# Results of the first four blocks copied out of PSUM by ScalarE, one block's taps back on VectorE, and the first loads in one ring

## The chip, the cores and the metric

The kernel runs on one core of one Trainium2 chip. The metric is the device time of one execution in microseconds (us); the kernel before has a median of 696.08 us in 5 runs (695.95 to 696.86). [...] Transfers issued by SP and ACT go through hardware queues, those issued by POOL through one software queue, called the ring here; all run on the core's 16 DMA engines.

## The reference

A light convolution along the sequence, then a two-layer network with exact GELU. Cut to what matters:

```
x: 8 x 4096 x 192;  weight: 8 heads x 7;  w_in: 192 x 2048;  w_out: 2048 x 192
w   = softmax(weight, over the 7 taps)
y[b, s, c] = sum over k of w[head(c), k] * x[b, s - 6 + k, c]     (zero before s = 0)
h   = y @ w_in                       (32768 tokens)
out = (0.5 * h * (1 + erf(h / sqrt 2))) @ w_out
```

## The kernel before

**Tiling.** The 32768 tokens are two halves of 16384, worked on side by side: the partitions 0 to 63 hold channels of the first half, 64 to 127 those of the second, and the 192 channels are three parts p of 64. Each half is cut into 34 blocks (`WS`): blocks 0 to 3 have 256 tokens of each half, blocks 4 to 33 have 512. Blocks are counted from 0 in this text. Matmuls come in pairs, one on each half of the rows of the array.

**A block's way.** (1) Four transfers (L182) bring x into `xin`, three buffers in turn. (2) VectorE transposes it into `xT`, three instructions (L390), and GpSimd copies the 6 tokens of overlap, the halo (L270, L281, L287). (3) The 7 taps: in most blocks VectorE takes them, 3 multiplications (L413) and 18 multiply-adds (L420), each over one p, the last three writing the bf16 tile `xc`. In the blocks listed in `PC` (0, 1 and 3) TensorE takes them instead, with diagonal matrices `dg`: `xT` is cast to bf16 (L502 on ScalarE for block 0, L365 on VectorE for blocks 1 and 3), 14 matmuls for each p (`pconv`, L564) add the taps in PSUM, and `xc` is copied from there (L510 on ScalarE for block 0, `conv_out`, L373, on VectorE for 1 and 3). (4) `mm1` (L602) multiplies `xc` by W_in into one of two PSUM tiles `hp`, one slice at a time: 8 slices in a block of 256, 16 in one of 512. (5) ScalarE applies GELU to each slice (L531) and writes `gT`. Slice u may enter its `hp` only after the GELU of slice u-2. (6) `mm2` (L636) multiplies `gT` by W_out into one of two PSUM tiles `ob`; a block is a row of units of two matmuls, 32 units to a group of 128 tokens per half: 64 units in a block of 256 tokens, 128 in one of 512. (7) `evac` (L429) on VectorE copies a finished group from `ob` to `osb`, 128x384 in f32, and SP stores it (L196).

**Order of the work.** It is written out by hand for each engine, and each engine works strictly in that order. TensorE goes through the slices of block n and, behind each slice, through some units of block n-1; the list `share` says how many for blocks 1 and 2, and elsewhere they are spread evenly. `behind` sets the `pconv` of block 1 behind slices 2, 4 and 6 of block 0, and that of block 3 behind slices 1, 2 and 3 of block 2. VectorE goes through 24 operations of each block (3 transposes, 21 taps); the list `side` puts other work in front of operation o of block b, written (b, o): the `conv_out` of block 1 at (2, 1), (2, 4) and (2, 8); transposes, casts and `conv_out` of block 3 in block 4; and each `evac`, for example that of block 0's first group at (2, 20). An `evac` waits for its group's last matmul, and what stands behind it on VectorE waits with it.

**The first loads.** SP loads half of block 0's x, ACT the other half; SP then waits for the first piece of W_in, loads half of block 1's x, waits for W_out, and loads blocks 3, 4 and so on. POOL's ring carries, in order: W_in's first quarter of a half (`win_in`, L236), then after an `affine_select` its second, the other half of block 1's x, then after the halo of block 0 the last piece of W_in, block 2's x, and W_out (L296). Each W_in piece fills one half of the partitions for its columns; `dup` (L350) on VectorE copies it to the other half. VectorE has `dup(0)`, `dup(1)`, the transposes and casts of block 1, then `dup(2)`, which slice 4 of block 0 needs.

The functions that the change touches, and what calls them:

## Time and profile before

| | |
|---|---|
| median of 5 runs | 696.08 us (695.95 to 696.86) |
| the profiled execution: its time | 696.08 us |
| its span in the profile | 694.2 us |
| TensorE clock granted | 1.00 |
| TensorE busy / ScalarE / VectorE | 685.6 / 528.3 / 552.7 us |
| HBM read / written | 52.92 / 25.17 MB |

The profile is of one execution. The span runs from its first to its last instruction; the execution's time holds 1.88 us more. A line such as "L531 ACT" is source line 531 on ScalarE; a row of the timeline gives start, length, engine, line, operation and count, and in brackets the idle time before it with what ended it. "x12" of L602 in a block of 256 tokens is one slice, "x6" in one of 512. The span of a group of matmuls there holds a tail that the next group overlaps; the chain of waits counts each stretch of time once, so lengths of TensorE's work are taken from the chain.

### The profile page before, as it was taken

How to read it: one execution, taken by the hardware profiler on the slowest of the kernel's cores; microseconds unless marked ns; L12 is line 12 of the kernel's file. 1: busy time of each engine (PE TensorE's matmuls, PEld its weight loads, DVE VectorE, ACT ScalarE, POOL GpSimd, SP SyncE). 2: the span in 40 equal slices, each digit the busy share in tenths (PEclk: the TensorE clock that was granted, in tenths of full speed). 3: DMA queues.
4: the chain of work that ended last, by engine and by line, in shares of the span. 5: the costliest groups of instructions: out<-in, count | busy, mean ns of one | idle time of the engine just before them, and what ended most of it. 6: DMA issues, size and time to landing. Idle time of an engine off the chain costs nothing.

```text
span 694.2 us, 25348 instructions
## 1 busy us (share of the span) xinstructions
PE 685.6 (99%) x11598; PEld 503.6 (73%) x11598; DVE 552.7 (80%) x915; ACT 528.3 (76%) x524; POOL 43.2 (6%) x93
## 2 busy tenths in 40 slices
PE   8899999999999999999999999999999999999997
PEld 4787677777777777777777777777777777777777
DVE  6898977789777889778898777898877898777811
ACT  6669877777777777777777777777777777777771
POOL 6100000000000000000000000000000000000000
PEclk9999999999999999999999999999999999999999
DMA  9858443445543355543355543355533455521013
GB/s 198 175 138 201 107 117 80 95 123 137 137 107 91 89 128 138 137 104 86 91 133 137 138 101 84 92 137 137 136 96 86 96 138 137 135 49 33 17 47 94
DMA packets 23082, 78.15 MB, mean 113 GB/s; under 512 B 6976, under 2 KB 11200, under 8 KB 19136
## 3 DMA queue, kind: packets, MB, share of 16 engines
q1 hardware_dynamic: 18640, 73.03, 44.0%
q0 software_dynamic: 3600, 2.73, 2.4%
q8 instruction: 91, 1.49, 0.9%
q10 hardware_dynamic: 736, 0.78, 0.4%
q14 instruction: 15, 0.12, 0.1%
HBM read 52.92 MB, written 25.17 MB: 112 GB/s over the span
## 4 chain that ended last, share of the span: by engine, by line
PE 96%; DMA 2%; DVE 1%; POOL 1%; ACT 0%; issue 0%
PE ob L636 49%; PE hp L602 47%; DMA xin<-in_x_dram 2%; PE ob L564 0%; ACT gT L531 0%; DVE xT L390 0%; POOL xin L182 0%; DVE acc L413 0%; POOL xTb L281 0%; POOL win L236 0%; ACT L488 0%; DVE acc L420 0%; DVE xc L373 0%; DVE osb L429 0%
## 5 line engine op out<-in xcount | busy, mean ns | idle before, releaser
L531 ACT ACTIVATE gT<-hp 128x1024 bf16<-128x1024 f32 x512 | 522.7, 1023 | 147.5 <-PE hp L602 147.3
L636 PEld LDWEIGHTS ob<-wout,gT 64*128 64x128 bf16 x8192 | 352.4, 94 | 115.7 <-PE ob L636 0.9
L636 PE MATMUL ob<-wout,gT 64*128 64x192 bf16 x8192 | 420.4, 243 | 0.2
L602 PE MATMUL hp<-xc,win 64*128 64x512 bf16 (+1 forms) x3264 | 415.1, 363 | 3.3 <-DVE xc L373 1.3
L420 DVE SCALAR_TENSOR_TENSOR acc<-xT,wcol,acc 128x512 f32<-128x512 f32 (+1 forms) x465 | 311.3, 732 | 0.0
L602 PEld LDWEIGHTS hp<-xc,win 64*128 64x128 bf16 x3264 | 150.1, 94 | 64.3 <-ACT gT L531 3.4
L429 DVE COPY osb<-ob 128x384 f32<-128x384 f32 x128 | 70.4, 550 | 130.9 <-PE ob L636 130.9
L390 DVE STREAM_TRANSPOSE xT<-xin 128x512 f32<-128x512 f32 (+1 forms) x102 | 61.2, 650 | 3.2 <-DMA xin<-in_x_dram 3.1
L420 DVE SCALAR_TENSOR_TENSOR xc<-xT,wcol,acc 128x512 bf16<-128x512 f32 (+1 forms) x93 | 63.4, 734 | 0.0
L287 POOL COPY xT<-xT 128x558 f32<-128x558 f32 x31 | 20.2, 652 | 578.5 <-DVE xT L390 578.5
L413 DVE TENSOR_SCALAR acc<-xT,wcol 128x512 f32<-128x512 f32 (+1 forms) x93 | 54.2, 633 | 1.1
L270 POOL COPY xT<-xT 128x18 f32<-128x18 f32 x28 | 11.5, 412 | 4.8 <-DVE xc L373 4.8
L564 PE MATMUL ob<-xTb,dg 64*64 64x256 bf16 x126 | 8.3, 272 | 0.3 <-ACT xTb L502 0.3
L564 PEld LDWEIGHTS ob<-xTb,dg 64*64 64x64 bf16 x126 | 6.3, 106 | 2.1 <-issue 1.1
L544 PE MATMUL hp<-warm 128*128 128x512 bf16 x16 | 5.9, 546 | 1.3 <-DVE warm L305 1.3
L544 PEld LDWEIGHTS hp<-warm 128*128 128x128 bf16 x16 | 2.0, 132 | 4.6 <-issue 3.0
L281 POOL CAST xTb<-xT 128x186 bf16<-128x186 f32 x9 | 3.4, 392 | 13.6 <-DVE xT L390 13.6
L236 POOL DMA_DIRECT2D win<-in_moe_w_in_dram x6 | 3.9, 659 | 0.8 <-POOLq L705 0.8
L350 DVE COPY win<-win 64x768 bf16<-64x768 bf16 (+1 forms) x6 | 3.4, 572 | 0.2
L502 ACT ACTIVATE xTb<-xT 128x256 bf16<-128x256 f32 x3 | 1.1, 416 | 2.6 <-DVE xT L390 2.6
L182 POOL DMA_DIRECT2D xin<-in_x_dram x6 | 3.0, 512 | 0.0
L373 DVE CAST xc<-ob 128x256 bf16<-128x256 f32 x6 | 2.5, 409 | 0.6 <-PE ob L564 0.6
(28 smaller groups left out, 14.5 us busy)
## 6 DMA issues: line engine op xcount, KB each, us to landing
xin<-in_x_dram SPq DMA_DIRECT2D x120, 380.0 KB, 6.6
out_dram<-osb SPq DMA_DIRECT2D x116, 192.0 KB, 3.1
out_dram<-osb SPq DMA_DIRECT2D x40, 48.0 KB, 2.2
xin<-in_x_dram SPq DMA_DIRECT2D x8, 188.0 KB, 3.7
xin<-in_x_dram POOLq DMA_DIRECT2D x6, 188.0 KB, 5.1
wout<-in_moe_w_out_dram POOLq DMA_DIRECT2D x1, 768.0 KB, 9.6
win<-in_moe_w_in_dram POOLq DMA_DIRECT2D x4, 96.0 KB, 4.4
win<-in_moe_w_in_dram POOLq DMA_DIRECT2D x2, 192.0 KB, 4.5
```

Source lines behind the costliest of these rows:

```text
L236: g.dma_start(ap(win, 64 * hf * NP * F + c0, [[NP * F, 64], [F, NP], [1, c1 - c0]]), ap(wint, hf * FH + c0, [[F, 64], [64 * F, NP], [1, c1 ...
L270: g.tensor_copy(dst, ap(xT[(n - 1) % 2], WS[n - 1] + 31, [[NP * XW, 128], [XW, NP], [32, HB]],),).then_inc(S_HALO)
L287: g.tensor_copy(ap(t, 1, [[NP * tw, 128], [tw, NP], [32, HB], [1, 31]]), ap(t, WS[n], [[NP * tw, 128], [tw, NP], [32, HB], [1, 31]]),).the ...
L390: v.transpose(ap(xT[n % 2], p * XW + HL, [[NP * XW, 128], [1, w]]), ap(xin[n % NX], 64 * p, [[TB // 32 * D, 128], [D, w // 32], [1, 32]],) ...
L413: ins = v.tensor_scalar(a, src, wk, None, ALU.mult)
L420: ins = v.scalar_tensor_tensor(dst, src, wk, a, op0=ALU.mult, op1=ALU.add)
L429: v.tensor_copy(ap(osb[m % 2], g * C, [[8 * C, 128], [4 * C, 2], [1, C]]), ap(ob[(G0[m] + g) % 2], 0, [[1024, 128], [512, 2], [1, C]]),).t ...
L531: a.activation(out=ap(gT[n % 2], i * c * 2 * w, dst), in_=ap(hp[u % 2], 0, src), func=AF.Gelu,).then_inc(S_GELU)
L544: t.matmul(hp[1][:, 0:512], warm[:, 0:128], warm[:, :])
L564: ins = t.matmul(b[r, o : o + w], dg[r, d0 : d0 + 64], xTb[PC[n]][r, x0 : x0 + w], start=(k == KS - 1), stop=(k == 0), tile_position=(64 * ...
L602: ins = t.matmul(hp[u % 2][:, hf * TB + cc * w : hf * TB + cc * w + w], win[r, p * F + wcols(hf, f0) : p * F + wcols(hf, f0) + 128], xc[n ...
L636: ins = t.matmul(ob[gg % 2][:, 512 * sub : 512 * sub + C], gT[m % 2][r, c0 : c0 + 128], wout[r, CH[i] * C : (CH[i] + 1) * C], start=(ph == ...
```

## The change

1. `PC` loses block 3: its taps are computed on VectorE like those of most blocks. Its `pconv`, casts and `conv_out` go, with TensorE's waits for them.
2. `evac` of blocks 0 to 3 (`NA = 4`, two groups each) moves from VectorE to ScalarE, as an `activation` with `Copy`, counted by a semaphore of its own, `S_EVA`. The dictionary `due` sets each in front of a GELU: group 0 of block 0 in front of slice (1, 6), group 0 of block m in front of the middle slice of block m+1, group 1 of block m in front of slice (m+2, 0). VectorE keeps `evac` from block 4 on.
3. The ring carries all of W_in first, behind the `affine_select` instead of partly ahead of it; then, after block 0's halo, half of block 1's x, block 2's x, W_out; then, after block 1's halo, block 3's x, which SP issued before. SP waits for block 3's x, not for W_out, and goes on with block 4.
4. `conv_out` of block 1 stands at (2, 1), (2, 5) and (2, 8).
5. The first slice of blocks 0 and 1 starts when parts 0 and 1 of `xc` are there; its matmuls on part 2 wait for part 2.
6. `share` of block 1 changes, so that units of block 0 start behind slice 2 instead of slice 3; that of block 2 goes, so that its units are spread evenly, 8 to a slice.

```diff
-    PC = {0: 0, 1: 1, 3: 2}
+    PC = {0: 0, 1: 1}
+    NA = 4
...
+        SW = {1: (2, 3), 2: (0, 2, 1, 3), 3: (0, 2, 1, 3)}
...
+        def evac(e, m, g):
+            e.wait_ge(S_MM2, G0[m] + g + 1)
+            if m >= 2 and g == 0:
+                e.wait_ge(S_OUT[m % 2], OUTS[m - 2])
+            dst = ap(osb[m % 2], g * C, [[8 * C, 128], [4 * C, 2], [1, C]])
+            src = ap(ob[(G0[m] + g) % 2], 0, [[1024, 128], [512, 2], [1, C]])
+            if m < NA:
+                e.activation(out=dst, in_=src, func=AF.Copy).then_inc(S_EVA)
+            else:
+                e.tensor_copy(dst, src).then_inc(S_EV)
...
-            win_in(FP[0], FP[1], S_WIN[0])
             g.wait_ge(S_MSET, 1)
...
-            win_in(FP[1], FP[2], S_WIN[1])
-            load(g, 1, (2, 3), S_XG[0])
+            for i in range(3):
+                win_in(FP[i], FP[i + 1], S_WIN[i])
...
             halo(0)
-            win_in(FP[2], FP[3], S_WIN[2])
-            load(g, 2, (0, 2, 1, 3), S_XG[1])
+            load(g, 1, SW[1], S_XG[1])
+            load(g, 2, SW[2], S_XG[2])
             g.dma_start(
                 ap(wout, 0, [[NF * C, 128], [C, NF], [1, C]]),
                 ap(woutt, 0, [[C, 128], [128 * C, NF], [1, C]]),
             ).then_inc(S_WOUT, 16)
-            for n in range(1, NB):
+            halo(1)
+            load(g, 3, SW[3], S_XG[3])
+            for n in range(2, NB):
                 halo(n)
...
+            side = [((2, 1 + (0, 4, 7)[p]), conv_out, 1, p) for p in range(NP)]
+            late = {}
...
+            due = {(1, 6): [(0, 0)]}
+            for m in range(NA):
+                if m >= 1:
+                    due[m + 1, NSL[m + 1] // 2] = [(m, 0)]
+                due[m + 2, 0] = [(m, 1)]
             for n in range(NB):
                 w = WS[n]
                 for i in range(NSL[n]):
+                    for k in due.get((n, i), []):
+                        evac(a, *k)
                     a.wait_ge(S_MM1, u + 1)
...
-                for n, i in ((1, 2 + 2 * p), (3, 1 + p)):
-                    behind[n - 1, i] = [(n, p, k) for k in range(KS - 1, -1, -1)]
+                behind[0, 2 + 2 * p] = [(1, p, k) for k in range(KS - 1, -1, -1)]
...
-                        t.wait_ge(S_PCE, pce(n, NP - 1))
+                        t.wait_ge(S_PCE, pce(n, NP - 2))
...
+                        if n in PC and i == 0 and cc == 0 and p == NP - 1:
+                            t.wait_ge(S_PCE, pce(n, p))
...
-            share = {1: [0, 0, 0, 11, 11, 10, 16, 16], 2: [7, 7, 6, 6, 6, 11, 11, 10]}
+            share = {1: [0, 0, 4, 10, 10, 8, 16, 16]}
...
-            sp.wait_ge(S_WOUT, 16)
-            load(sp, 3)
+            sp.wait_ge(S_XG[3], 64)
```

## The prediction

> **What bounds the kernel.** I read the page's first part, then the waits, the chain in order of time, and the timeline of the first 75 us.

> ```profile
> PE 685.6 (99%) x11598; PEld 503.6 (73%) x11598; DVE 552.7 (80%) x915; ACT 528.3 (76%) x524; POOL 43.2 (6%) x93
> ```

> TensorE (PE) is busy for 99% of the span. The waits (waiter, released by: us in total, times, longest) show where it is not:

> ```profile
> ACT gT L531 <- PE hp L602: 147.3, 489, 1.4
> DVE osb L429 <- PE ob L636: 130.9, 42, 4.7
> ...
> PEld hp L602 <- ACT gT L531: 3.4, 4, 1.6
> DVE xT L390 <- DMA xin<-in_x_dram: 3.1, 2, 1.8
> ...
> PE hp L602 <- DVE xc L373: 1.3, 1, 1.3
> ```

> ScalarE and VectorE wait for TensorE, hundreds of times; TensorE waits for them a handful of times, and the timeline has all of these before 25 us. So the time is a start with holes, then TensorE's work without holes. A change gains by less work for TensorE, or by filling holes before 25 us; it loses where it makes TensorE wait. The chain (start, length, what) shows both:

> ```profile
> 11.00 5.98 DMA xin<-in_x_dram
> ...
> 24.28 0.83 PE hp L602 x12
> 25.11 0.91 PE ob L636 x22
> ...
> 35.14 0.88 PE ob L564 x14
> ...
> 39.73 0.88 PE ob L564 x14
> ```

> Block 2's x lands late (16.98) and holds VectorE, behind whose transposes block 1's conv_out stands; then two GELUs; from 24.28, slice (1, 3), TensorE runs without a break. The L564 lines, with a third at 37.36, are block 3's taps.

> **Block 3's taps leave TensorE.** Three pieces of 0.88 us on an unbroken path: -2.64 us. Nothing waits in their place unless xc of blocks 3, 4 or 5 is late; that is counted below.

> **The start.** All of W_in now goes ahead of block 1's x, so slice (0, 4), which needs dup(2), hangs on block 1's x alone. The timeline rows:

> ```profile
> 8.25 1.26 POOL L236 DMA_DIRECT2D win<-in_moe_w_in_dram  x2
> ...
> 9.50 1.99 POOL L182 DMA_DIRECT2D xin<-in_x_dram  x4
> ...
> 11.48 1.20 POOL L296 DMA_DIRECT2D wout<-in_moe_w_out_dram  x1
> 11.54 1.10 DVE L390 STREAM_TRANSPOSE xT<-xin 128x256 f32<-128x256 f32 x3 [1.28 <-DMA xin<-in_x_dram]
> ...
> 15.31 0.83 PE L602 MATMUL hp<-xc,win 64*128 64x256 bf16 x12 [0.45 <-DVE win L350]
> ```

> POOL's halo of block 0 ends at 8.30 in both kernels: without the wait of the old order the affine_select (0.56) can run at 1.3 and the three win issues (1.39, 1.29, 1.26) end by 5.9. Behind the halo, half of block 1's x is issued at 8.3 and 8.8 instead of 4.58 and 5.1. From issue to landing, x transfers took 2.7 to 4.7 us on ACT's and SP's queues before 8 us and 4.3 to 6.0 on POOL's. I take 3.7, that of SP's half of block 1 at 7.0, because by 10 us the ring has nothing ahead of it (it moved 0.20 MB in the us from 6 to 7, so W_in's 0.77 MB take 4 us from 4.7 on): 12.5 (11.5 at 2.7, 14.8 at 6.0), against 11.52 before. Transposes, casts and dup(2) then take 3.79 as before (11.52 to 15.31), so slice (0, 4) starts at 16.3. From there the rows of before give slice (0, 7)'s GELU 4.82 later (20.13 - 15.31), two more GELUs at 0.97 (22.29 to 24.24) and 1.02 for the last to end: slice (1, 3) at 16.3 + 7.8 = 24.1. Before it was 24.28, held by conv_out. Block 2's x no longer waits behind W_in's last piece in the ring, is issued 0.2 earlier and lands by 17.0 or sooner; VectorE, done with dup(2) at 16.2, takes it at once, and conv_out's last part waits for pconv to 20.5, no longer for x. Gain 0.15. The new share puts 4 units behind slice (1, 2), in the wait for a GELU: 8 matmuls, 0.33 by the chain's 0.66 for 16. Together -0.48; with 11.5 for the landing it is -1.5, with 14.8 it is +1.8. The split wait of slice (0, 0) saves the time of 4 matmuls (0.22), which is lost again in the wait for dup(2): nothing. W_out must be there at 23.8; it landed near 21.5, by SP's wait of 13.3 us from 8.2, and is now issued a little earlier.

> **ScalarE's copies.** The trace has no ScalarE copy of 384 elements into f32. The nearest rows are Copy of 256 (L510, 383 ns) and GELU of 1024 (L531, 1023 ns); on the line between them 384 elements take 0.49, and successive rows start 0.1 before the last one ends (11.23 and 12.15), so one copy holds ScalarE for 0.4. In blocks 1 to 3 a slice lasts 1.31 with its 8 units and ScalarE idles 0.29 in it; TensorE may be two slices ahead, 2.62, of which matmul (0.85) and GELU (1.02) take 1.87. So 0.75 of slack hides each copy. In block 4 only 4 units follow a slice:

> ```profile
> 58.42 16.66 ACT L531 ACTIVATE gT<-hp 128x1024 bf16<-128x1024 f32 x17 [0.28 <-PE hp L602]
> ```

> 17 GELUs start 0.9775 apart without a gap, the slack of two slices is 1.955 - 1.87 = 0.08, and two copies fall here. Block 2's second group comes in front of slice (4, 0), partly in the gap of 0.28: 0.1. Block 3's first group comes in front of (4, 8): 0.4 less the slack, 0.3. What TensorE loses here it doesn't get back. +0.4; at 0.28 a copy (the row of 256, overlapped) +0.2, at 0.92 (the row of 1024) +1.5. Below nothing is excluded: ScalarE gets only more work. Behind each copy on ScalarE stand all later GELUs, and for these TensorE waits.

> [...]

> **VectorE.** It gains 3 + 18 taps of 256 and loses 3 casts, 3 conv_outs and 8 copies with their waits. The row "21.19 4.83 ... x12" gives 0.40 a tap. Before, block 2's taps would have ended at 27.8 without the wait for the copy at 29.34 (idle 3.32); now 0.35 earlier, since the last conv_out stands 0.35 earlier: 27.4. Block 3: transposes 1.1, halo 0.3, taps 3 x 0.3 + 18 x 0.4 = 8.1; 36.9. A block of 512 without copies took 15.6 (block 5 from 53.65 to 72.11, less two copies of 0.56 and their waits of 1.24 and 0.51). Block 4 is done at 52.5, block 5 at 68.1. TensorE wants block 4 at 57.57 - 2.64 - 0.48 = 54.45 and block 5 at 73.21 - 2.72 = 70.5. So VectorE has 1.9 and 2.4 us to spare: nothing. If the cover went, each late us would be a us of time. Later blocks take VectorE 16.9 of 20.9 us, so it only gets further ahead.

> POOL's four issues of block 3's x (0.5 each) stand ahead of halo(2); behind block 1's halo they are done by 17, and the halo is wanted after 18. SP's wait moves the load of block 4 by less than 2 us; block 4 is transposed at 37.

> **Sum.** -2.64 - 0.48 + 0.4 = -2.72, from the profiled execution's 696.08 (span 694.2 and 1.88 around it), which is also the median: 693.4.

> [...] The rows first: POOL issued W_in's last piece at 8.25 while VectorE ran dup's bf16 copies (8.13 to 10.26), and its two issues took 1.26, no more than the 1.29 and 1.39 of the others. [...]

> **Rivals.** (a) *The start gains nothing or loses.* One ring serves block 1's x after 768 KB of other work; landing at 14 instead of 12.5 gives -2.64 + 1.0 + 0.4 = -1.2, 694.9. For it: POOL's own rows reach 6.0. Against: those were behind W_in's last piece. (b) *VectorE becomes the wall*: at 0.47 a tap (L420's mean of 256) blocks 2 and 3 last 2.5 longer, block 4 is 0.6 late, block 5 is not: 694.0. Against: the rows overlap, 12 in 4.83. [...] (d) *More than forecast*: x lands at 11.5, -3.7: 692.4.

> **Chances.** Forecast 0.63; (a) 0.14; (b) 0.10; (c) 0.06; (d) 0.07. A change below 0.2% (1.4 us) can't be told from none. Forecast, (b) and (d) are faster, 0.80; (a) the same, 0.14; slower 0.06. The range reaches from the best of (d) with the cheap copy, 692.2, over (a) and the dear copy (-1.6, 694.5) to 695.2; the rest of (a) and (c) stay out.

> **What would show it.** Right: no L564 after 25 us; slice (1, 3) near 24.1; ACTIVATE rows osb<-ob of about 0.49; a wait of PE for ACT near 62 after the span's start, of 0.3; block 4's first slice with no wait for VectorE. Wrong: a DVE wait for x beyond 13 ahead of the second set of transposes, a wait of PE for W_out near 24, or PE waiting for DVE xc at blocks 3, 4 or 5.

## The result, and the profile after

The changed kernel takes 694.25 us (median of 24 runs, 693.03 to 696.96) against 696.12 (46 runs of the kernel before, 695.19 to 697.41, made beside them): the ratio is 0.9974, 95% interval 0.9968 to 0.9979. So it is faster, by 1.9 us, where 2.7 was forecast. The runs of the kernel after fall in two groups by TensorE's granted clock: of 25 executions 8 were granted 0.999 to 1.000 over the span and took 693.03 to 693.88, and 17 were granted 0.995 to 0.998 and took 694.09 to 696.96. In the profiled execution of the kernel before, the clock was 1.00.

The profiled execution took 695.21 us (span 693.3, clock 0.997), 0.87 less than the profiled one of before. The first part of its page and the row of the new copies (PE is TensorE, DVE VectorE, ACT ScalarE, POOL GpSimd, SP SyncE):

```profile
PE 684.4 (99%) x11556; PEld 503.8 (73%) x11556; DVE 554.4 (80%) x922; ACT 530.9 (77%) x532; POOL 44.5 (6%) x95
...
L194 ACT ACTIVATE osb<-ob 128x384 f32<-128x384 f32 x8 | 3.9, 486 | 0.3 <-PE ob L647 0.3
```

TensorE lost 42 matmuls, block 3's taps, but its busy time fell by 1.2 us only, not by 2.64: something in it became longer. The waits (waiter, released by: us in total, times, longest):

```profile
DVE xT L413 <- issue: 3.8, 1, 3.8
...
PE ob L576 <- DVE xTb L388: 2.3, 1, 2.3
```

The last line is new: TensorE waits 2.3 us for block 1's casts. The wait for block 1's `conv_out` (1.3 before) is gone. The chain (start, length, what) shows what the casts hung on:

```profile
7.62 4.47 DMA xin<-in_x_dram
12.09 1.81 issue
13.90 1.10 DVE xT L413 x3
15.28 0.95 PE ob L576 x14
16.23 2.58 PE hp L615 x24
...
20.18 1.42 PE hp L615 x24
```

Block 1's x reaches VectorE at 13.90 instead of 11.54. At 16.23 two slices of block 0 take 2.58, where the next two, at 20.18 in the same chain, take 1.42. The columns that matter in the table of windows are the first (from:to in us), TensorE's busy time with its matmuls in brackets, and, third from the end, the granted clock:

```profile
16.00:17.00 1.00, 1.00 (x16) 0.68 (x12) 0.97 (x2) 0.00 (x0) 1.00 (x2) 0.69 1.59 191
17.00:18.00 1.00, 1.00 (x14) 0.55 (x10) 0.97 (x4) 0.50 (x1) 0.74 (x3) 0.50 1.61 203
...
19.00:20.00 1.00, 1.00 (x14) 0.78 (x10) 0.78 (x2) 0.87 (x1) 0.37 (x1) 0.61 1.51 298
```

The kernel before, in the same us:

```profile
17.00:18.00 1.00, 1.00 (x22) 0.90 (x22) 0.99 (x3) 0.38 (x2) 0.00 (x0) 1.00 1.60 192
```

After the idle 2.3 us TensorE is granted half its clock (0.50), from about 16.4 to 19.8: it is "busy" in every us, with two thirds of the matmuls (14 from 17 to 18 instead of 22). That is where a busy time hides a loss. From there the two kernels can be laid beside each other by the start of the first slice of each block. The timeline's rows for blocks 2 and 3, before and then after:

```profile
33.09 0.82 PE L602 MATMUL hp<-xc,win 64*128 64x256 bf16 x12
...
47.05 0.82 PE L602 MATMUL hp<-xc,win 64*128 64x256 bf16 x12
```

```profile
34.79 0.82 PE L615 MATMUL hp<-xc,win 64*128 64x256 bf16 x12
...
45.31 0.82 PE L615 MATMUL hp<-xc,win 64*128 64x256 bf16 x12
```

| first slice of block | before | after | lead of after | what changed it |
|---|---|---|---|---|
| 2 | 33.09 | 34.79 | -1.70 | the start, forecast +0.48 |
| 3 | 47.05 | 45.31 | +1.74 | block 2 is 3.44 shorter, forecast 2.64 |
| 4 | 57.57 | 56.35 | +1.22 | a pause of TensorE near 49.5, not foreseen |
| 5 | 73.21 | 72.36 | +0.85 | block 4 is 0.37 longer, forecast 0.4 |

From block 5 on nothing moves: 0.85 is the difference of the spans (694.2 and 693.3).

### The profile page after: what moved, and what is told of

Read it like the earlier page. It is cut to its first block, busy times and chain, and to the rows that moved or that the text cites. A ratio compares the mean times of both kernels' runs of the same rounds, so it can differ in the third digit from the quotient of the medians.

```text
span 693.3 us, 25405 instructions
## 1 busy us (share of the span) xinstructions
PE 684.4 (99%) x11556; PEld 503.8 (73%) x11556; DVE 554.4 (80%) x922; ACT 530.9 (77%) x532; POOL 44.5 (6%) x95
## 4 chain that ended last, share of the span: by engine, by line
PE 95%; ACT 2%; DMA 1%; issue 1%; DVE 0%; POOL 0%; SPq 0%
PE ob L647 48%; PE hp L615 47%; ACT gT L547 2%; DMA win<-in_moe_w_in_dram 1%; DMA xin<-in_x_dram 1%; PE ob L576 0%; DVE xT L413 0%; ACT osb L194 0%; POOL win L258 0%; DVE osb L196 0%; POOL idb L266 0%; SPq L204 0%; DVE warm L328 0%; DVE xTb L388 0%; DVE idb L329 0%
## 5 line engine op out<-in xcount | busy, mean ns | idle before, releaser
L547 ACT ACTIVATE gT<-hp 128x1024 bf16<-128x1024 f32 x512 | 522.8, 1023 | 143.6 <-PE hp L615 143.6
L443 DVE SCALAR_TENSOR_TENSOR acc<-xT,wcol,acc 128x512 f32<-128x512 f32 (+1 forms) x480 | 316.9, 725 | 0.0
L196 DVE COPY osb<-ob 128x384 f32<-128x384 f32 x120 | 66.1, 551 | 126.7 <-PE ob L647 126.7
L308 POOL COPY xT<-xT 128x558 f32<-128x558 f32 x32 | 20.9, 652 | 588.3 <-DVE xT L413 588.3
L291 POOL COPY xT<-xT 128x18 f32<-128x18 f32 x29 | 11.5, 396 | 3.6 <-DVE xc L396 3.6
L576 PE MATMUL ob<-xTb,dg 64*64 64x256 bf16 x84 | 5.8, 287 | 2.5 <-DVE xTb L388 2.3
L576 PEld LDWEIGHTS ob<-xTb,dg 64*64 64x64 bf16 x84 | 4.6, 114 | 4.0 <-DVE xTb L388 2.6
L204 POOL DMA_DIRECT2D xin<-in_x_dram x10 | 5.1, 519 | 0.0
L194 ACT ACTIVATE osb<-ob 128x384 f32<-128x384 f32 x8 | 3.9, 486 | 0.3 <-PE ob L647 0.3
L373 DVE COPY win<-win 64x768 bf16<-64x768 bf16 (+1 forms) x6 | 3.2, 526 | 0.2
L510 ACT ACTIVATE xTb<-xT 128x256 bf16<-128x256 f32 x3 | 1.1, 416 | 2.7 <-DVE xT L413 2.7
```

What stands on the lines that cost most here:

```text
L196: e.tensor_copy(dst, src).then_inc(S_EV)
L204: e.dma_start(ap(xin[n % NX], 32 * q * (TB // 32 * D), [[TB // 32 * D, 32], [1, mb * D - 32]],), ap(xt, off, [[mb * D, 32], [1, mb * D - 3 ...
L291: g.tensor_copy(dst, ap(xT[(n - 1) % 2], WS[n - 1] + 31, [[NP * XW, 128], [XW, NP], [32, HB]],),).then_inc(S_HALO)
L308: g.tensor_copy(ap(t, 1, [[NP * tw, 128], [tw, NP], [32, HB], [1, 31]]), ap(t, WS[n], [[NP * tw, 128], [tw, NP], [32, HB], [1, 31]]),).the ...
L443: ins = v.scalar_tensor_tensor(dst, src, wk, a, op0=ALU.mult, op1=ALU.add)
L547: a.activation(out=ap(gT[n % 2], i * c * 2 * w, dst), in_=ap(hp[u % 2], 0, src), func=AF.Gelu,).then_inc(S_GELU)
```

## The experiments

The theory after the result (A): the landing of block 1's x is set by the 16 transfer engines, which have W_in's last piece to move first; the late x makes TensorE idle, and the idle costs the clock; block 2 gained more than its taps because its units are now spread evenly; ScalarE's copies cost 0.37 in block 4. Rivals: the late x is a matter of POOL's queue (its latency or its later issue); the lower clock has nothing to do with the idle time; the even spread is worth nothing.

**1. The ring in its old order.** Everything else as in the kernel after.

```diff
+            win_in(FP[0], FP[1], S_WIN[0])
             g.wait_ge(S_MSET, 1)
...
-            for i in range(3):
-                win_in(FP[i], FP[i + 1], S_WIN[i])
+            win_in(FP[1], FP[2], S_WIN[1])
+            load(g, 1, SW[1], S_XG[1])
...
             halo(0)
-            load(g, 1, SW[1], S_XG[1])
+            win_in(FP[2], FP[3], S_WIN[2])
```

> The changed kernel with the old order of W_in and block 1's x in the ring (half of block 1's x ahead of W_in's last piece, the first piece ahead of the affine_select); all else as changed. Theory A (the start lost 1.7 us: block 1's x landed at 13.85 instead of 11.5, and after TensorE's idle 2.3 us its clock was lowered for a while, 1.1 us of it): block 1's x at 11.5, clock 1.000 in all runs, slice (1, 3) near 24.3 with 4 units of mm2 ahead of it, time 692.3 to 693.0. Rival B (the start is no worse than before; the loss against the forecast sits in ScalarE's copies or in block 4): within 0.3 of the changed kernel's 694.25.

Measured: 692.84 us (692.22 to 693.45), 0.995 of before (0.9938 to 0.9963), clock 0.999 to 1.000 in every run. VectorE's row of block 1's transposes (start, length, and in brackets the wait):

```profile
11.64 1.10 DVE L414 STREAM_TRANSPOSE xT<-xin 128x256 f32<-128x256 f32 x3 [1.29 <-DMA xin<-in_x_dram]
```

x is there 2.3 earlier, and the whole kernel is 1.4 us faster by the medians. The new order of W_in and block 1's x, a piece of part 3 of the change, is a loss inside this kernel. TensorE now waits 0.75 for block 1's `conv_out` before 21.86 (1.33 in the kernel before).

**2. TensorE kept busy.** The ring as in the kernel after; ten matmuls of zeros behind slice (0, 2) fill the idle time.

```diff
                     mm1(n, i)
+                    if (n, i) == (0, 2):
+                        for _ in range(10):
+                            t.matmul(ob[1][:, 512:1024], warm[:, 0:128], warm[:, :])
```

> The changed kernel with 10 matmuls of zeros behind slice (0, 2), into a part of PSUM that is free then, so that TensorE does not idle while block 1's x is late. Theory A (the lowered clock costs 1.1 us on top of the late x): clock 1.000 in all runs, the two slices at 16.2 take 1.5 instead of 2.65, time 693.2 to 693.6, as in those runs of the changed kernel that have clock 1.000, and a smaller spread. Rival B (those matmuls are slow for another reason, transfers or weight loads): 694.2 or more, with the same slow slices.

Measured: 693.33 us (693.13 to 694.11), 0.996 (0.9948 to 0.9973), clock 1.000 in all five runs. The useless matmuls and the two slices behind them (TensorE's timeline), and a window that had 0.50 in the kernel after:

```profile
13.46 2.10 PE L672 MATMUL ob<-warm 128*128 128x512 bf16 x9 [0.16 <-issue]
...
16.39 1.48 PE L615 MATMUL hp<-xc,win 64*128 64x256 bf16 x24
```

```profile
17.00:18.00 1.00, 1.00 (x20) 0.74 (x18) 1.00 (x4) 0.74 (x1) 0.42 (x2) 1.00 1.56 185
```

x is nearly as late as in the kernel after (13.58), the two slices take 1.48 instead of 2.65 in the timeline, and the kernel gains 0.9 by the medians, by doing more work. That the lower clock comes of the idle time is shown: nothing else was changed, and 17 of 25 executions had lost the clock without these matmuls.

**3. Block 2's units as they were.**

```diff
-            share = {1: [0, 0, 4, 10, 10, 8, 16, 16]}
+            share = {1: [0, 0, 4, 10, 10, 8, 16, 16], 2: [7, 7, 6, 6, 6, 11, 11, 10]}
```

> The changed kernel with the old uneven list of mm2 units behind block 2's slices (7, 7, 6, 6, 6, 11, 11, 10 instead of 8 each). Theory A (block 2 got 3.44 us shorter, from 13.96 to 10.52, of which 2.64 are the taps; the other 0.8 come from mm2 runs that are no longer cut at the change of phase, where the next matmul waits for the last): block 2 takes 11.2 to 11.3, time 0.7 to 0.8 above the changed kernel: 695.0. Rival B (the 0.8 belong to the taps, to TensorE's switching to them and back): block 2 stays at 10.5, time unchanged at 694.25.

Measured: 694.99 us (11 runs, 693.96 to 696.71), 0.9982 (0.9973 to 0.9991): 0.74 more than the kernel after by the medians. Compared at the same clock it is 0.6 to 0.7: 693.96 and 694.07 against a median of 693.44 at full clock, medians of 695.09 against 694.39 below it. Block 2 lasts 11.11 on TensorE (slices 34.63 to 45.74), against 10.52 after and 13.96 before. So of the 3.44 the even spread is 0.59; the other 2.85 are the taps, with whatever else of the change bears on block 2. The chain of this run shows a place where the difference arises:

```profile
36.68 0.58 PE ob L647 x14
37.26 0.66 PE hp L615 x12
37.92 0.18 PE ob L647 x4
38.10 0.05 issue
38.15 0.51 PE ob L647 x8
```

Fourteen matmuls in one go take 0.58, so twelve should take 0.50; here they are cut after the first four and take 0.74. The like happens at 43.28 to 44.43 (22 in 1.15 instead of 0.91). The waits between 33 and 48 us name what is waited for:

```profile
PEld ob L647 <- PE ob L647: 0.6, 2, 0.3
```

TensorE waits for itself. `mm2` works each group of 32 units in two phases of 16, and the first matmul of the second phase waits, by the kernel's semaphore `S_PH`, for the last one of the first. With the old list the 16th and the 48th unit of block 2 fall in the middle of a stretch, and the wait is open; the kernel before has the same two waits there. With 8 units behind every slice, a phase always ends where a slice of `mm1` follows, and the kernel after has no such wait in block 2. Two waits of 0.24 make 0.48 of the 0.59.

**4. The ring's change alone.** The kernel before, with W_in ahead of block 1's x.

```diff
-            win_in(FP[0], FP[1], S_WIN[0])
             g.wait_ge(S_MSET, 1)
...
-            win_in(FP[1], FP[2], S_WIN[1])
-            load(g, 1, (2, 3), S_XG[0])
+            for i in range(3):
+                win_in(FP[i], FP[i + 1], S_WIN[i])
...
             halo(0)
-            win_in(FP[2], FP[3], S_WIN[2])
+            load(g, 1, (2, 3), S_XG[0])
```

> The kernel before with one thing changed: W_in's three pieces go ahead of block 1's x in the ring, behind the affine_select. Theory A: block 1's x lands at 13.9, TensorE idles 2.3 us and its clock falls below 1.000 in most runs; slice (1, 3) starts 1 to 2 us later than 24.28; time 697.1 to 698.1. Rival B (block 1's x late is hidden behind block 2's x, which held block 1's conv_out before): 696.1 within 0.3.

Measured: 698.84 us (698.28 to 700.35), 1.0043 (1.003 to 1.0055), clock 0.994 to 0.998 in every run.

```profile
14.35 1.10 DVE L389 STREAM_TRANSPOSE xT<-xin 128x256 f32<-128x256 f32 x3 [4.16 <-issue]
```

x comes at 14.35, TensorE idles 2.42, and the kernel loses 3.0 us (0.43% of 696). The part that the prediction counted as a gain is a loss from both sides: put in, it costs 3.0; taken out (run 1), it returns 1.4 by the medians. Why it costs twice as much in this kernel is open; x is 0.45 later here than in the kernel after, and in the profiled execution, the slowest of the five, the half clock lasted at least 6.2 us (a mean of 0.70 from 14 to 16, 0.50 from there to 21) instead of 3.41.

**5. Three blocks on ScalarE instead of four** (on top of run 1). The copies of block 3, which fall among block 4's GELUs, go back to VectorE.

```diff
-    NA = 4
+    NA = 3
...
-            late = {}
+            late = {(3, 0): (5, 15), (3, 1): (6, 1)}
```

> The kernel of the run with the old ring order (692.84), with ScalarE copying the results of three blocks instead of four: block 3's two groups go back to VectorE at (5, 15) and (6, 1). Theory A (ScalarE's copy in front of slice (4, 8) costs 0.3, since block 4 leaves no slack there): the 0.35 that TensorE's weight load waits for a GELU near 64 is gone, block 4 lasts 15.65 instead of 15.95, time 692.5. Rival B (TensorE would have lost this time in block 4 anyway, by another wait): block 4 stays at 15.95. VectorE has time for both: it is done with block 5 about 2 us ahead.

Measured: 691.93 us (691.56 to 692.69), 0.9935 (0.9923 to 0.9946). TensorE's rows of the first slices of blocks 4 and 5:

```profile
53.80 0.81 PE L616 MATMUL hp<-xc,win 64*128 64x512 bf16 x6
...
69.44 0.81 PE L616 MATMUL hp<-xc,win 64*128 64x512 bf16 x6
```

Block 4 lasts 15.64, as before the change; in run 1 it lasted 15.94 (54.10 to 70.04) and in the kernel after 16.01. So the copy in front of slice (4, 8) costs 0.30 to 0.37, and the one in front of (4, 0), which run 5 keeps, nothing. The medians of runs 5 and 1 differ by 0.9, more than the traces show; they come from two comparisons, and the intervals of their ratios overlap.

**6. All of block 1's x by SP** (the ring as after, but without block 1's x).

```diff
-        SW = {1: (2, 3), 2: (0, 2, 1, 3), 3: (0, 2, 1, 3)}
+        SW = {2: (0, 2, 1, 3), 3: (0, 2, 1, 3)}
...
-            load(g, 1, SW[1], S_XG[1])
...
-            load(sp, 1, (0, 1))
+            load(sp, 1)
```

> The changed kernel with all four parts of block 1's x on SP's queue, behind the same wait for W_in's first piece; the ring carries W_in, block 2's x, W_out, block 3's x. Theory A (the 5.0 us from issue to landing belong to POOL's queue, which begins to move data only 2 us after the issue, and to the x of block 2 right behind): SP issues at 7.3 to 8.6 and block 1's x lands at 12.4 to 12.9, about 1 us sooner than 13.85; TensorE idles 1 us less, the clock stays at 1.000 in most runs, time 692.6 to 693.3. Rival B (the wire is full until then, whoever issues): 13.5 or later and 694.2 as in the changed kernel.

Measured: 695.73 us (12 runs, 692.73 to 697.8), 0.9988 (0.9974 to 1.0002): by the medians slower than the kernel after, though the two intervals overlap. This was a miss of theory A as I had put it before this run, which still gave POOL's queue a latency of its own.

```profile
14.93 1.10 DVE L412 STREAM_TRANSPOSE xT<-xin 128x256 f32<-128x256 f32 x3 [5.08 <-DMA xin<-in_x_dram]
```

x is a full us later, although SP issued all of it by 9. Between 8 and 14 us the kernel after moves 206 to 247 GB/s and this one 210 to 265, but for one us in each with more. Here block 2's x, next in the ring, takes its share of the engines while block 1's x is still on the way. The queues between 12 and 13 us (packets, MB, share; q1 carries SP's transfers, q0 the ring's):

```profile
q1 hardware_dynamic: 32, 0.13, 50.1%
q0 software_dynamic: 30, 0.12, 48.8%
```

So SP's queue did not bring x sooner, and what else is under way counts. That the ring has no delay of its own is not shown, because block 2's x moved up as block 1's left the ring. TensorE idled 3.54 us, and 11 of the 12 runs were granted less than the full clock.

**7. Block 1's x ahead of W_in** (on top of run 6). SP issues it right behind block 0's.

```diff
             load(sp, 0, (0, 1))
-            sp.wait_ge(S_WIN[0], 32)
             load(sp, 1)
```

> As the last one, but SP issues block 1's x right behind block 0's, without the wait for W_in. Theory A (block 1's x is what slice (0, 4), TensorE's idle time and its clock hang on): x lands near 8, the dup of W_in's last piece, which lands near 11 to 12, becomes the last, slice (0, 4) starts at 13.5 to 14.5, block 2's x lands by 15 to 16 and no longer holds conv_out, slice (1, 3) starts near 22.5 instead of 24.28; clock 1.000, time 690.5 to 691.3. Rival B (W_in's first piece, pushed back by block 1's x, now holds slice (0, 0)): 692.5 or more.

Measured: 693.04 us (692.5 to 693.98), 0.9951 (0.9938 to 0.9963). Now W_in's first piece is late, and with it the first slice:

```profile
12.19 3.67 PE L614 MATMUL hp<-xc,win 64*128 64x256 bf16 x36 [2.41 <-DVE win L372]
```

The first 36 matmuls start 2.3 later than after, take 3.67 where 2.22 would do by the row of run 2 (24 in 1.48), and the clock falls again in this execution (0.997 over the span): a hole of 2.41 in another place. What is issued first decides which of the two is late. It costs less here: only two of six runs lost the clock, and the median is 2.7 below run 6 and 1.2 below the kernel after.

**8. Run 7 with three blocks on ScalarE** (`NA = 3` and `late` as in run 5).

> The last one and block 3's results copied by VectorE again. Theory A: a further 0.3 less than the last one, 690.2 to 691.0, unless VectorE is now late for block 4, whose slices come sooner. Rival B (VectorE, whose slack the earlier start uses up, holds block 4 or 5): no better than the last one, with TensorE waiting for DVE xc near 52 or 68.

Measured: 693.51 us (692.23 to 694.09), 0.9952 (0.9937 to 0.9967). Inconclusive: four of six runs had the lower clock. The two at full clock took 692.23 and 692.27, the four of run 7 692.5 to 693.04.

**9. `conv_out` of block 1 earlier** (on top of run 5).

```diff
-            side = [((2, 1 + (0, 4, 7)[p]), conv_out, 1, p) for p in range(NP)]
+            side = [((2, (0, 1, 5)[p]), conv_out, 1, p) for p in range(NP)]
```

> The best kernel so far (old ring order, ScalarE copies for three blocks, 691.93) with block 1's conv_out one place sooner on VectorE: (2, 0), (2, 1), (2, 5) instead of (2, 1), (2, 5), (2, 8). Theory A (in that kernel slice (1, 0) waits 0.8 for the last conv_out, which stands behind block 2's transposes and these behind its x, landing at 17.3): the last conv_out ends near 20.2 instead of 21.5, slice (1, 0) follows slice (0, 7) at once, slice (1, 3) comes 0.6 sooner, time 691.3. Rival B (the GELUs of block 0's last slices hold the same slices anyway): gain under 0.2, 691.8.

Measured: 691.71 us (691.55 to 692.41), 0.9939 (0.9926 to 0.9951). Slice (1, 3) starts at 23.94 instead of 24.30: TensorE's wait of 0.83 for `conv_out` is gone. Some 0.34 of it doesn't show, because slice (0, 4), which stands ahead of all that the edit touches, began 0.34 later in this execution (16.10 against 15.76). In time it can't be told from run 5. These two are the best versions of the study, 4.2 to 4.4 us below the kernel before.

**10. Only W_in's last piece back in its place.** The first two stay ahead of block 1's x, as in the kernel after.

```diff
-            for i in range(3):
+            for i in range(2):
                 win_in(FP[i], FP[i + 1], S_WIN[i])
+            load(g, 1, SW[1], S_XG[1])
...
             halo(0)
-            load(g, 1, SW[1], S_XG[1])
+            win_in(FP[2], FP[3], S_WIN[2])
```

> The changed kernel with half of block 1's x back in front of W_in's last piece in the ring; the first piece stays behind the affine_select, and all else as changed. Theory A (the transfer engines move a fixed 0.2 to 0.25 MB a us from 4.7 on, and block 1's x waits for the 0.38 MB of W_in's last piece and then for its own): x lands near 11.7 instead of 13.85, the clock stays at 1.000, time 692.6 to 693.1, like the run with the whole old order (692.84). Rival B (what matters is the first piece, 0.6 later behind the affine_select, which holds SP's wait and so SP's half of block 1's x): x lands at 13 or later, time above 693.6.

Measured: 692.35 us (692.08 to 692.45), 0.9945 (0.9932 to 0.9959), clock 1.000 in every run.

```profile
11.72 1.10 DVE L414 STREAM_TRANSPOSE xT<-xin 128x256 f32<-128x256 f32 x3 [1.56 <-DMA xin<-in_x_dram]
```

So it is the order of W_in's last piece and block 1's x that makes x late. Moving the first piece behind the `affine_select`, the other half of the ring's change, does no harm. Two things come with that order: the bytes ahead of x, and its issue, which stands ahead of block 0's halo here (4.47) and behind it in the kernel after (8.30). A run with x behind all of W_in but ahead of the halo would separate them; there is none.

## Why the prediction was right in its number and wrong in a step

The direction and the range (692.2 to 695.2) held, and in the 8 executions at full clock the median is 693.4, the very forecast. It is no proof of the working: two misses nearly cancel there. The start is 1.1 worse than forecast even at full clock (+0.6 instead of -0.48), and block 2 is 0.8 better (-3.44 instead of -2.64). That they are of like size is luck.

- **The taps (-2.64): right, a little small.** Run 3 gives 2.85 with the old spread of units. The rest fits units that take longer right behind a tap: 14 matmuls take 0.68 there in the chain of before (36.02), and 0.58 in that of run 3. No tap of block 3 is left on TensorE, and nothing waits in its place.
- **The even spread of block 2 (no term): missed.** Part 6 of the change was listed and never costed. It is worth 0.59 (run 3), a fifth of the whole forecast.
- **The start (-0.48): wrong, +1.70.** The step that failed is "From issue to landing ... I take 3.7". The ring's half of block 1's x was issued at 8.30 and 8.8 as worked out, but landed 4.6 and 5.0 later, and VectorE had x at 13.90, not 12.5. The 3.7 is a number of SP's queue, though the ring's own rows for the same two transfers were at hand. The first of the two (count, KB, median us from issue to landing), before and after:

```profile
xin<-in_x_dram POOLq DMA_DIRECT2D x1, 188.0 KB, 4.3
```

```profile
xin<-in_x_dram POOLq DMA_DIRECT2D x1, 188.0 KB, 4.6
```

  With the ring's 4.3 to 4.7 of before, the landing would have been put at 13.1 to 13.5. The reason given for 3.7, that the ring has nothing ahead of it by 10, looked at one queue. W_in went on to about 9.6; from 9 to 11 SP's half (0.39 MB) passed over the same engines, and the ring's half came with it and behind it. How much of the 4.6 and 5.0 is this traffic and how much the ring's own delay no run separates (runs 6 and 10). The condition of rival (a), a landing at 14, came true.
- **The clock (no term): missed, and the larger part of the 1.70.** In run 2, with the clock kept and x at 13.58, slice (1, 3) starts at 24.88, 0.60 later than before, of which 0.33 are the units in front that before stood behind it; that is a start 0.27 later. With x 0.32 later still, as after, it is 0.6. The other 1.1 of the 1.70 is the clock. In the trace of before TensorE waited 1.33 us at most after its first matmul and the clock stayed at 1.00, so no row warned of it; but a forecast that makes TensorE wait longer than any row of the trace should say that the clock is unknown there. My rivals with a late x priced the wait alone.
- **ScalarE's copies (+0.4): right.** A copy takes 486 ns (0.49 forecast). Block 4 grew by 0.37; of the two copies there, forecast at 0.1 and 0.3, the first costs nothing (run 5). The mechanism is the one named: at 65.0, where 62 was forecast, the chain shows a copy between two GELUs, and TensorE waiting for the second:

```profile
65.02 0.49 ACT osb L194
65.51 0.92 ACT gT L547
66.43 0.05 issue
66.48 0.82 PE hp L615 x6
```

- **VectorE (nothing): right.** Block 4's taps end at 54.3, wanted at 56.35; block 5's at 69.8, wanted at 72.36. That is 1.7 to 1.8 later than forecast, but the late start held TensorE up by as much. No wait of TensorE for `xc` of blocks 3, 4 or 5 is in the trace. Rival (b) is out.
- **POOL's issues beside VectorE's copies: not stretched.** The first issues of POOL's x run beside `dup`'s copies (8.18 to 10.06), the last behind them, and the six take 0.49 each (0.51 in the trace of before):

```profile
8.30 2.95 POOL L204 DMA_DIRECT2D xin<-in_x_dram  x6
```

The 0.06 of (c), a slower kernel, stood on a stretch of these issues, which no run shows; that x was 1.4 late has another cause.

In the profiled execution the terms are -3.44 + 1.70 + 0.37 and a pause of about 0.5 near 49.5, in sum -0.87. The pause stays open: TensorE stands still in block 3 with nothing shown as its releaser. Pauses of 0.2 to 0.8 are also in the traces of runs 2, 4 and 6, at other places, and none in runs 1, 3, 5 and 10. At full clock the 1.1 falls away: the 8 executions that had it lie at 693.0 to 693.9.

## What to carry to other kernels

For the time from issue to landing take the row of the same transfer on the same queue (here 4.3 to 4.7), not that of another queue (3.7), and count what all queues have under way: run 6 put x on another queue and got it a us later. Here a piece that nobody needed yet (W_in's last) stood in front of the one that TensorE waited for. A wait at the start of a kernel can cost twice: behind the 2.3 us here TensorE had half its clock for 3.41 us, which cost 1.1 us more, and its busy share (99%) doesn't show it; look at the granted clock of the run and at the matmuls per us. And cost every listed part of a change, a reordered list as well: the even spread is worth 0.59, by moving a wait of TensorE for its own result to where other work covers it.

## What the runs showed of the hardware that was not expected

**Useless work can pay.** Ten matmuls of zeros in the hole took the kernel from 694.25 to 693.33 us, and in five runs none lost the clock.
